# Gating the w_in quarters on early loads, moving the scalars to ScalarE's queue, moving column sum and bias add to GpSimd, and scheduling for longer DMA transposes in a fused linear-attention and StarReLU kernel

## Chip, cores and metric

One core of one Trainium2 chip. The metric is the device time of one execution in microseconds (us). "Fast" and "slow" are states of a run: a run is called slow when it is over 1.5% above the fastest of the same kernel.

## The reference, cut

```python
for t in range(S):                      # B, H, S, D = 4, 8, 768, 48
    state = alpha[:, :, t, :, None] * state + k_t (outer) v_t
    y[:, :, t] = q_t @ state
x = y.transpose(0, 2, 1, 3).reshape(B * S, H * D)        # 3072 x 384
h = x @ w_in                                              # 384 -> 2048
g = s * relu(h) ** 2 + b
out = g @ w_out                                           # 2048 -> 384
```

## The kernel before

The 3072 rows are 24 blocks of 128. Per block: alpha, q, k, v are loaded, log decay is summed on TensorE (PE), q and k are scaled and transposed, scores are masked, and y is formed and transposed into `xd`. Blocks are gathered in groups; a unit is one PSUM bank of up projection (`mm1`) or a quarter of a block's down projection (`mm2`). Both s and b stay out of the big products: `oevac` multiplies by s and adds `bias_w`, which is b times the column sum of w_out.

A list scheduler in Python, with assumed durations, decides the order in which every engine's instructions are emitted. The engines then run in that order. The parts that matter:

```python
GROUPS = [1, 1, 2, 2, 2, 4, 4, 4, 4]     # blocks per group
LEAD = 24.0                              # how far attention runs ahead, in units
N_PE_T = 10                              # blocks 0..9 transpose on PE, the rest by DMA
LOADS = ["b0", "i0", "i1", "b1", "i2", "i3", "b2", "o0", "o1", "o2", "o3", "b3"]
...
def colsum_part(i):
    nc.vector.tensor_tensor(out=colpart if i else colsum, ...)   # 128x768 float32
...
# scalars b and s: issued on GpSimd's DMA queue, behind the four w_in quarters
op("POOL", 0.7, t + 30, lambda: nc.gpsimd.dma_start(out=b_col, ...), w=["b"], lat=2.0)
op("POOL", 0.8, -5, bias_mul, r=["b"], w=["bones"])
...
# DMA transposes of q and k, and of y, with the scheduler's assumed times
op("SP", 0.5, -3000, st_Tdma, n, r=[("qb", i3), ("kb", i3)], w=[("qkT", i3)], lat=1.2, dma=1.1)
op("SP", 0.5, -3000, st_yTdma, n, r=[("yn", i3)], w=[xd], lat=1.2, dma=0.5)
...
op("DVE", 0.54, t + 0.1, oevac, x, r=[o, "bias", "s"], w=[("os", (x // 4) % 3)], drop=o)
```

## Time and profile before

| | before |
|---|---|
| time, median (3 runs) | 205.95 us (205.75 to 206.21) |
| span of the profiled run | 204.4 us |
| PE busy / idle | 167.6 / 36.8 us |
| DVE, ACT, POOL busy | 131.7, 107.8, 39.7 us |

PE idle of a stretch is its length minus PE's busy time there; the prediction gives it by stretch. DVE is VectorE, ACT ScalarE, POOL GpSimd, SP SyncE.

### The profile page before, as it was taken

To read this page: it belongs to the slowest core of one execution; us is meant where nothing else is said; L and a number is where in the kernel's file an instruction comes from. 1 tells how busy PE (TensorE), PEld (TensorE's weight loads), DVE (VectorE), ACT (ScalarE), POOL (GpSimd) and SP (SyncE) were. 2 spreads that over 40 slices of the span, in tenths; PEclk is the share of its full clock that TensorE was granted. 3 is DMA by queue.
4 is the path that set the end of the run, shared out by engine and by line. 5 is a ranking of instruction groups with operands and counts; after the bars stand their busy time and mean duration, and the time that the engine had idled before them with its cause. 6 is when DMAs were issued, how large, how long until landed. Compare 5 with 4: busy or idle time off the path is not lost.

```text
span 204.4 us, 4279 instructions
## 1 busy us (share of the span) xinstructions
PE 167.6 (82%) x1594; PEld 107.4 (53%) x1594; DVE 131.7 (64%) x240; ACT 107.8 (53%) x235; POOL 39.7 (19%) x76
## 2 busy tenths in 40 slices
PE   1301966897999999897789978897969999999993
PEld 0201954656887887663355544454536555555661
DVE  3501299979999998967567857776757544444321
ACT  4100689836897677643746856557445444444100
POOL 8403034124104530031223100321202000000000
PEclk9999999999999999999999999999999999999999
DMA  6999999999999999999999799999964221111122
GB/s 131 175 189 195 270 379 209 188 209 227 189 211 188 216 205 191 188 211 178 159 224 184 148 204 206 176 204 209 201 138 109 61 59 40 40 42 38 38 77 77
DMA packets 127701, 33.64 MB, mean 165 GB/s; under 512 B 121024, under 2 KB 127680, under 8 KB 127680
## 3 DMA queue, kind: packets, MB, share of 16 engines
q1 hardware_dynamic: 126016, 31.80, 75.3%
q0 software_dynamic: 1664, 1.57, 4.8%
q8 instruction: 12, 0.20, 0.4%
q14 instruction: 9, 0.07, 0.1%
HBM read 25.17 MB, written 4.72 MB: 146 GB/s over the span
## 4 chain that ended last, share of the span: by engine, by line
PE 56%; DMA 26%; DVE 7%; issue 4%; POOL 3%; ACT 3%; SPq 0%; POOLq 0%; ACTq 0%; DVEq 0%
PE bank L530 23%; PE bank L502 22%; DMA qkT<-qk 19%; DMA b_col<-in_moe_b_dram 6%; PE a_ps L417 3%; PE bank L353 2%; POOL w_in_bf L255 2%; DMA a_in<-in_alpha_dram 1%; PE bank L450 1%; DVE colpart L272 1%; DVE am L426 1%; PE bank L309 1%; PE bank L376 1%; ACT r L511 1%; DVE gt L523 1%
## 5 line engine op out<-in xcount | busy, mean ns | idle before, releaser
L502 PE MATMUL bank<-xd,w_in_bf 128*128 128x512 bf16 (+2 forms) x432 | 76.5, 315 | 0.7 <-DMA xd<-yn 0.5
L511 ACT ACTIVATE r<-bank 128x512 bf16<-128x512 f32 x96 | 56.6, 604 | 35.7 <-PE bank L502 26.7
L530 PE MATMUL bank<-w_out_bf,gt 128*128 128x384 bf16 x384 | 73.7, 326 | 0.0
L523 DVE TENSOR_TENSOR gt<-r 128x512 bf16<-128x512 bf16 x96 | 41.9, 448 | 23.7 <-ACT r L511 23.3
L530 PEld LDWEIGHTS <-gt 128*128 128x128 bf16 x384 | 35.7, 98 | 25.3 <-issue 0.2
L502 PEld LDWEIGHTS <-w_in_bf 128*128 128x128 bf16 x432 | 38.2, 101 | 18.8 <-issue 1.4
L426 DVE TENSOR_TENSOR am<-a_ps,mask 128x1024 bf16<-128x1024 f32 x24 | 29.3, 1219 | 11.7 <-PE a_ps L417 11.5
L406 POOL TENSOR_TENSOR s_st<-t,blast 64x192 bf16<-64x192 bf16 x32 | 19.3, 603 | 43.7 <-PE bank L442 11.7
L330 POOL CAST vb<-v_in 128x384 bf16<-128x384 f32 x24 | 13.1, 546 | 61.3 <-DMA v_in<-in_v_dram 29.8
L539 DVE SCALAR_TENSOR_TENSOR o_sb<-bank,s_col,bias_w 128x384 f32<-128x384 f32 x24 | 14.7, 613 | 13.9 <-PE bank L530 13.9
L302 ACT ACTIVATE la<-a_in 128x384 bf16<-128x384 f32 x24 | 12.7, 530 | 18.4 <-DMA a_in<-in_alpha_dram 18.4
L463 ACT ACTIVATE yn<-bank 128x384 bf16<-128x384 f32 x24 | 11.9, 496 | 17.8 <-PE bank L450 17.7
L417 PE MATMUL a_ps<-qkT 64*128 64x128 bf16 x192 | 9.7, 222 | 10.6 <-DMA qkT<-qk 9.1
L333 DVE TENSOR_TENSOR qk<-q_in,b_s 128x384 bf16<-128x384 f32 x24 | 13.9, 579 | 4.3 <-ACT b_s L323 4.3
L323 ACT ACTIVATE b_s<-bank 128x384 f32<-128x384 f32 x24 | 11.8, 491 | 7.5 <-PE bank L314 6.8
L376 PE MATMUL bank<-vb,qk 128*128 128x96 bf16 x80 | 6.8, 209 | 10.7 <-POOL vb L330 10.7
L341 DVE TENSOR_TENSOR qk<-k_in,binv 128x384 bf16<-128x384 f32 x24 | 14.4, 598 | 0.4 <-DMA k_in<-in_k_dram 0.4
L417 PEld LDWEIGHTS <-qkT 64*128 64x128 bf16 x192 | 5.5, 95 | 15.7 <-DMA qkT<-qk 12.0
L309 PE MATMUL bank<-la,U_bf 128*128 128x384 bf16 x24 | 8.2, 340 | 4.9 <-ACT la L302 4.9
L450 PE MATMUL bank<-vb,am 128*128 128x48 bf16 x192 | 8.9, 185 | 3.8 <-DVE am L426 3.8
L326 ACT ACTIVATE binv<-bank 128x384 f32<-128x384 f32 x24 | 11.9, 494 | 0.0
L376 PEld LDWEIGHTS <-qk 128*128 128x128 bf16 x80 | 4.9, 99 | 12.8 <-issue 10.8
(42 smaller groups left out, 106.5 us busy)
## 6 DMA issues: line engine op xcount, KB each, us to landing
a_in<-in_alpha_dram SPq DMA_DIRECT2D x24, 192.0 KB, 3.8
q_in<-in_q_dram SPq DMA_DIRECT2D x24, 192.0 KB, 3.7
k_in<-in_k_dram SPq DMA_DIRECT2D x24, 192.0 KB, 3.7
v_in<-in_v_dram SPq DMA_DIRECT2D x24, 192.0 KB, 3.8
out_dram<-o_sb SPq DMA_DIRECT2D x24, 192.0 KB, 2.2
wst<-in_moe_w_out_dram SPq DMA_DIRECT2D x4, 768.0 KB, 8.3
w_in_bf<-in_moe_w_in_dram POOLq DMA_DIRECT2D x4, 384.0 KB, 9.5
qkT<-qk SPq DMA_TRANSPOSE x14, 3.8
```

The costliest lines, as they stand in the source:

```text
L330: nc.gpsimd.tensor_copy(out=vb_sb[n % 3], in_=v_in[n % NIN])
L333: nc.vector.tensor_tensor(out=qk_sb[n % 3][:, 0, :, 0:D], in0=q_in[n % NIN], in1=b_sb[n % 2], op=ALU.mult,)
L341: nc.vector.tensor_tensor(out=qk_sb[n % 3][:, 1, :, 0:D], in0=k_in[n % NIN], in1=binv_sb[n % 2], op=ALU.mult,)
L376: nc.tensor.matmul(out=p_ps[:, p, :], lhsT=kb[:, 128 * p : 128 * p + 128], rhs=vb[:, 96 * p : 96 * p + 96], start=True, stop=True,)
L406: nc.gpsimd.tensor_tensor(out=s_sb[n % 2][rows, :, cols], in0=t1_sb[n % 2][rows, :, cols], in1=blast_sb[n % 2][rows].unsqueeze(2).to_broad ...
L417: nc.tensor.matmul(out=a_ps[:, e, p, :], lhsT=qkT[64 * e : 64 * e + 64, 1, p, :], rhs=qkT[64 * e : 64 * e + 64, 0, p, :], start=True, stop ...
L426: nc.vector.tensor_tensor(out=am_sb[n % 2].rearrange("a e p t -> a (e p) t"), in0=a_ps.rearrange("a e p t -> a (e p) t"), in1=mask.unsquee ...
L502: nc.tensor.matmul(out=hp[:, i * n : (i + 1) * n], lhsT=w_in_bf[:, kk, 128 * j : 128 * (j + 1)], rhs=xd_sb[g % 3][:, kk, 0:n], start=(kk = ...
L511: nc.scalar.activation(out=r_sb[w % 2], in_=bank("h", w), func=AF.Relu)
L523: nc.vector.tensor_tensor(out=dst, in0=r, in1=r, op=ALU.mult)
L530: nc.tensor.matmul(out=op[:, 0:d_model], lhsT=gt_sb[:, slot, j, :], rhs=w_out_bf[:, j, :], start=(j == 0), stop=(j == NJ - 1),)
L539: nc.vector.scalar_tensor_tensor(out=out_sb[(x // 4) % 3], in0=bank("o", x // 4)[:, 0:d_model], scalar=s_col, in1=bias_w, op0=ALU.mult, op ...
```

## The change

The intent is to fill PE's empty start: let the narrow loads that attention needs go first, let w_in follow when they have landed, take the scalars out of w_in's queue, unload DVE, and let the scheduler assume longer DMA transposes. Two more blocks are transposed on PE, and one group of two blocks becomes two groups of one. The diff, cut:

```diff
-GROUPS = [1, 1, 2, 2, 2, 4, 4, 4, 4]
-LEAD = 24.0
+GROUPS = [1, 1, 2, 1, 1, 2, 4, 4, 4, 4]
+LEAD = 28.0
-N_PE_T = 10
+N_PE_T = 12
+AFTER = ['k0', 'q1', 'k2', 'k2']
+N_POOL_BIAS = 12
+NOUT = 4
+TLAT = 3.0
-LOADS = ["b0", "i0", "i1", "b1", "i2", "i3", "b2", "o0", "o1", "o2", "o3", "b3"]
+LOADS = 'a0 q0 k0 v0 a1 q1 k1 v1 a2 q2 k2 a3 q3 k3 v2 v3 o0 o1 o2 o3 a4 q4 k4 v4'
...
+    nc.scalar.dma_start(out=b_col, in_=moe_b.to_broadcast((128, 1)))
+    nc.scalar.dma_start(out=s_col, in_=moe_s.to_broadcast((128, 1)))
...
+    def touch(what):                       # waits on GpSimd for a load
+        src = tensors[what[0]][1][what[1]]
+        nc.gpsimd.tensor_copy(out=touch_sb, in_=src[:, 0, 0:1])
...
-        nc.vector.tensor_tensor(            # column sum
+        nc.gpsimd.tensor_tensor(
...
+    def oscale(x): nc.scalar.activation(out=out_sb[...], in_=bank("o", x // 4)[...], func=AF.Copy, scale=s_col)
+    def obias(x): nc.gpsimd.tensor_tensor(out=o_sb, in0=o_sb, in1=bias_w, op=ALU.add)
...
+        op("POOL", 0.06, -3000 + i, touch, x, r=[x], w=[("touch", i)])
+        op("POOL", 0.9, -3000 + i, load_w_in, i, r=[("touch", i)], w=[("wib", i)], lat=1.2, dma=2.3)
...
-                   lat=1.2, dma=1.1)        # st_Tdma
+                   lat=TLAT, dma=1.6)
-                op("SP", 0.5, -3000, st_yTdma, n, r=[("yn", i3)], w=[xd], lat=1.2, dma=0.5)
+                op("SP", 0.5, -3000, st_yTdma, n, r=[("yn", i3)], w=[xd], lat=TLAT, dma=0.7)
```

The first 12 evacuations become `oscale` and `obias`; the other 12 stay on DVE. The rest of the diff adds a fourth output buffer and tunes assumed durations and the scheduler's own model of the queues.

More of the change, by code (lines that the diff above doesn't have):

```diff
@@ L81, in run, with since, u_eng @@
         until = {}
-        queue = 0.0
+        queue = soft = 0.0
+        flying = []
         todo = n
+        def since(u):
+            a = 0.0
+            for d in self.ops[u][5]:
+                same = self.ops[d][0] == self.ops[u][0]
+                x = end[d] + (0.0 if same and u_eng(u) == "PE" else self.ops[d][6])
+                a = max(a, x + (0.0 if same and self.ops[d][7] is None else self.HOP))
+            return a
+        def u_eng(u):
+            return self.ops[u][0]
         def start(a, i):
@@ L108, in run @@
                 free[e] = end[i] = t + dur
+            elif eng == "POOL":
+                free[e] = t + dur
+                at = max(t + 1.3, soft)
+                soft = end[i] = at + dma
+                flying = [x for x in flying if end[x] > at]
+                for x in flying:
+                    end[x] += dma
+                queue = max(queue, at) + dma
+                for e2, items in ready.items():
+                    ready[e2] = [(since(x), x) for _, x in items]
             else:
@@ L111, in run @@
                 end[i] = queue
+                flying.append(i)
                 free[e] = max(t + dur, queue - self.BACKLOG)
@@ L127, in run @@
                 if not left[u]:
-                    a = 0.0
-                    for d in self.ops[u][5]:
-                        same = self.ops[d][0] == self.ops[u][0]
-                        x = end[d] + (0.0 if same and eng == "PE" else self.ops[d][6])
-                        a = max(a, x + (0.0 if same else self.HOP))
-                    ready[self.ops[u][0]].append((a, u))
+                    ready[u_eng(u)].append((since(u), u))
         self.begin, self.end = begin, end
@@ L235 @@
     gt_sb = sb.tile([128, RING, NJ, C], BF16, name="gt")
-    out_sb = many("o_sb", 3, [128, d_model], FP32)
+    out_sb = many("o_sb", NOUT, [128, d_model], FP32)
     w_in_bf = sb.tile([128, 3, d_ff], BF16, name="w_in_bf")
@@ L243 @@
     colpart = sb.tile([128, 2 * d_model], FP32, name="colpart")
+    touch_sb = sb.tile([128, 1], FP32, name="touch")
     bones = sb.tile([128, 128], FP32, name="bones")
@@ L279, in colsum_add @@
     def colsum_add():
-        nc.vector.tensor_tensor(out=colsum, in0=colsum, in1=colpart, op=ALU.add)
+        nc.gpsimd.tensor_tensor(out=colsum, in0=colsum, in1=colpart, op=ALU.add)
     def bias_mul():
@@ L539, in oevac @@
         nc.vector.scalar_tensor_tensor(
-            out=out_sb[(x // 4) % 3],
+            out=out_sb[(x // 4) % NOUT],
             in0=bank("o", x // 4)[:, 0:d_model],
@@ L549, in ostore, with oscale, obias @@
         n = x // 4
-        nc.sync.dma_start(out=out[n * C : (n + 1) * C, :], in_=out_sb[(x // 4) % 3])
+        nc.sync.dma_start(out=out[n * C : (n + 1) * C, :], in_=out_sb[(x // 4) % NOUT])
+    def oscale(x):
+        nc.scalar.activation(
+            out=out_sb[(x // 4) % NOUT],
+            in_=bank("o", x // 4)[:, 0:d_model],
+            func=AF.Copy,
+            scale=s_col,
+        )
+    def obias(x):
+        o_sb = out_sb[(x // 4) % NOUT]
+        nc.gpsimd.tensor_tensor(out=o_sb, in0=o_sb, in1=bias_w, op=ALU.add)
     sched = Schedule(len(banks), {"c": 2, "T": 1, "P": 2, "y": 2, "Y": 1, "h": 3, "o": 2, "b": 1})
@@ L557, in want @@
         return (4 * n - LEAD) * UNIT
-    loads = LOADS + [f"b{n}" for n in range(NBLK) if f"b{n}" not in LOADS]
-    early = {0: [], 1: []}
-    for rank, item in enumerate(loads):
-        t, i = rank - 1000, int(item[1:])
-        if item[0] == "i":
-            op("POOL", 0.9, t, load_w_in, i, w=[("wib", i)], lat=1.2, dma=2.3)
-        elif item[0] == "o":
-            op("SP", 0.5, t, load_w_out, i, w=[("wst", i)], lat=1.2, dma=2.2)
+    loads = LOADS.split()
+    for n in range(NBLK):
+        loads += [x for x in (f"{y}{n}" for y in "aqkv") if x not in loads]
@@ L567 @@
+    tensors = {"a": (alpha, a_in), "q": (q, q_in), "k": (k, k_in), "v": (v, v_in)}
+    ranks = {}
+    for rank, item in enumerate(loads):
+        x, i = item[0], int(item[1:])
+        ranks[x, i] = rank - 1000
+        if x == "o":
+            op("SP", 0.5, rank - 1000, load_w_out, i, w=[("wst", i)], lat=1.2, dma=2.2)
             for e in range(2):
                 op("ACT", 0.78, -400, cast_w_out, i, e, r=[("wst", i)], w=[("wob", i, e)])
-            op("DVE", 0.85, -5, colsum_part, i, r=[("wst", i)],
+            op("POOL", 1.3, -2, colsum_part, i, r=[("wst", i)],
@@ L570 @@
                w=["colpart" if i else "colsum"])
             if i:
-                op("DVE", 0.85, -5, colsum_add, r=["colpart"], w=["colsum"])
-        elif i == 0:
-            for x, (name, src, dst) in enumerate(
-                (("a", alpha, a_in), ("q", q, q_in), ("k", k, k_in), ("v", v, v_in))
-            ):
-                op("SP", 0.45, t + 0.1 * x, load, 0, src, dst, w=[(name, 0)], lat=1.2, dma=0.98)
-            op("POOL", 0.7, t + 30,
-               lambda: nc.gpsimd.dma_start(out=b_col, in_=moe_b.to_broadcast((128, 1))),
-               w=["b"], lat=2.0)
-            op("POOL", 0.7, t + 30,
-               lambda: nc.gpsimd.dma_start(out=s_col, in_=moe_s.to_broadcast((128, 1))),
-               w=["s"], lat=2.0)
-            op("POOL", 0.8, -5, bias_mul, r=["b"], w=["bones"])
+                op("POOL", 1.3, -2, colsum_add, r=["colpart"], w=["colsum"])
@@ new lines, in block_loads @@
+    def block_loads(n):
+        for x, (src, dst) in tensors.items():
+            op("SP", 0.45, ranks[x, n], load, n, src, dst, w=[(x, n % NIN)], lat=1.2, dma=0.98)
+    for n in range(4):
+        block_loads(n)
+    for i in range(4):
+        x = AFTER[i][0], int(AFTER[i][1:])
+        op("POOL", 0.06, -3000 + i, touch, x, r=[x], w=[("touch", i)])
+        op("POOL", 0.9, -3000 + i, load_w_in, i, r=[("touch", i)], w=[("wib", i)], lat=1.2, dma=2.3)
+    op("POOL", 0.8, -5, bias_mul, r=[("S", 0)], w=["bones"])
@@ L595 @@
             t = want(n)
-            if n:
-                rank = loads.index(f"b{n}") - 1000
-                for x, (name, src, dst) in enumerate(
-                    (("a", alpha, a_in), ("q", q, q_in), ("k", k, k_in), ("v", v, v_in))
-                ):
-                    op("SP", 0.45, rank + 0.1 * x, load, n, src, dst, w=[(name, ii)],
-                       lat=1.2, dma=0.98)
+            if n >= 4:
+                block_loads(n)
             op("ACT", 0.43, t - 1.0, st_ln, n, r=[("a", ii)], w=[("la", i2)])
@@ L608 @@
             op("POOL", 0.6, t + 0.2, st_vcast, n, r=[("v", ii)], w=[("vb", i3)])
-            op("DVE", 0.47, t + 0.2, st_qb, n, r=[("q", ii), ("b", i2)], w=[("qb", i3)])
-            op("DVE", 0.47, t + 0.2, st_kb, n, r=[("k", ii), ("bi", i2)], w=[("kb", i3)])
+            op("DVE", 0.52, t + 0.2, st_qb, n, r=[("q", ii), ("b", i2)], w=[("qb", i3)])
+            op("DVE", 0.52, t + 0.2, st_kb, n, r=[("k", ii), ("bi", i2)], w=[("kb", i3)])
             if n < N_PE_T:
@@ L613 @@
                    take=("T", n))
-                op("DVE", 0.61, t + 0.4, st_Tcopy, n, r=[("T", n)], w=[("qkT", i3)], drop=("T", n))
+                op("DVE", 0.66, t + 0.4, st_Tcopy, n, r=[("T", n)], w=[("qkT", i3)], drop=("T", n))
             else:
                 op("SP", 0.5, -3000, st_Tdma, n, r=[("qb", i3), ("kb", i3)], w=[("qkT", i3)],
-                   lat=1.2, dma=1.1)
+                   lat=TLAT, dma=1.6)
             if not last:
@@ L628 @@
             op("PE", 0.33, t + 0.5, st_A, n, r=[("qkT", i3)], w=["a"], lat=0.27)
-            op("DVE", 1.15, t + 0.6, st_mask, n, r=["a"], w=[("am", i2)])
+            op("DVE", 1.2, t + 0.6, st_mask, n, r=["a"], w=[("am", i2)])
             rr = [("am", i2), ("qkT", i3), ("vb", i3)] + ([] if first else [("S", 1 - i2)])
@@ L646 @@
             t = w * UNIT
-            op("PE", 0.66, t, mm1, w,
+            op("PE", {1: 0.76, 2: 0.71, 4: 0.66}[m], t, mm1, w,
                r=[("xd", g % 3, x) for x in range(m)] + [("wib", j0 // 4)],
                w=[("h", w)], lat=0.27, take=("h", w))
-            op("ACT", 0.5, t + 0.5, relu, w, r=[("h", w)], w=[("r", w % 2)], drop=("h", w))
+            op("ACT", 0.51, t + 0.5, relu, w, r=[("h", w)], w=[("r", w % 2)], drop=("h", w))
             op("DVE", 0.36, t + 1.0, square, w, r=[("r", w % 2)],
@@ L663 @@
             if jq == 3:
-                op("DVE", 0.54, t + 0.1, oevac, x, r=[o, "bias", "s"],
-                   w=[("os", (x // 4) % 3)], drop=o)
-                op("SP", 0.5, -2000, ostore, x, r=[("os", (x // 4) % 3)], dma=0.55)
+                os = ("os", (x // 4) % NOUT)
+                if x // 4 < N_POOL_BIAS:
+                    op("ACT", 0.38, t + 0.1, oscale, x, r=[o], w=[os], drop=o)
+                    op("POOL", 0.7, t + 0.1, obias, x, r=["bias"], w=[os])
+                else:
+                    op("DVE", 0.58, t + 0.1, oevac, x, r=[o, "bias"], w=[os], drop=o)
+                op("SP", 0.5, -2000, ostore, x, r=[os], dma=0.55)
     sched.emit()
```

## The prediction

> **What bounds the kernel now.** I began with the page's first part. TensorE (PE) is busy 167.6 us of a 204.4 us span and its clock is granted in full, so the span is 167.6 us of PE work plus 36.8 us in which PE stands still. No other engine comes near (VectorE, DVE, has 131.7 us). The question is therefore where those 36.8 us lie and which of them the change takes away.
>
> Second, the table of busy time in stretches of 5 us (columns: stretch, its length, then PE, PEld, DVE, ACT, POOL busy with counts, granted clock, DMA share, GB/s):
>
> ```profile
> 5.00:10.00 5.00, 1.68 (x16) 1.13 (x17) 2.94 (x4) 0.79 (x3) 2.63 (x5) 1.00 1.12 175
> 10.00:15.00 5.00, 0.00 (x0) 0.00 (x0) 0.00 (x0) 0.00 (x0) 0.00 (x0) 1.00 1.21 189
> 15.00:20.00 5.00, 0.80 (x12) 0.66 (x11) 0.26 (x1) 0.04 (x1) 1.58 (x3) 1.00 1.04 194
> ...
> 70.00:75.00 5.00, 5.00 (x58) 3.97 (x57) 5.00 (x9) 3.36 (x9) 2.79 (x6) 1.00 0.97 209
> ...
> 100.00:105.00 5.00, 3.49 (x29) 1.80 (x28) 3.06 (x6) 2.03 (x4) 0.67 (x2) 1.00 1.09 202
> ...
> 165.00:170.00 5.00, 5.00 (x29) 2.62 (x28) 2.23 (x5) 2.20 (x5) 0.00 (x0) 1.00 0.11 41
> ```
>
> Adding five minus PE busy over all stretches gives PE idle of 17.0 us in 0 to 20, 6.6 us in 20 to 50, 0 in 50 to 85, 9.8 us in 85 to 155 and 3.5 us after that (the last evacuation and store). The reader should see that from 10 to 15 us every engine is idle while the DMA engines are full. The tail from 155 is pure PE work, so time saved earlier arrives at the end almost one for one.
>
> Third, the chain of waits says why (start, length, what):
>
> ```profile
> 6.29 11.52 DMA b_col<-in_moe_b_dram
> 17.99 0.61 POOL bones L284
> 18.60 0.48 POOL vb L330
> 19.12 0.48 PE bank L376 x4
> ...
> 38.06 0.88 DVE colpart L272
> 38.96 0.97 DVE colsum L280
> 40.06 1.53 PE bank L290 x4
> ```
>
> A load of 0.5 KB, the scalar b, takes 11.5 us. GpSimd (POOL) waits for it in program order to scale `bones`, and the cast of v for block 0 stands behind that. Later the column sum on DVE, seven instructions of about 0.94 us, ends at 39.9 us and PE waits for it before the bias matmul.
>
> Fourth, the DMA view of single issues in that stretch (last column: us from issue to landing):
>
> ```profile
> v_in<-in_v_dram SPq DMA_DIRECT2D x1, 192.0 KB, 6.0
> w_in_bf<-in_moe_w_in_dram POOLq DMA_DIRECT2D x1, 384.0 KB, 6.6
> a_in<-in_alpha_dram SPq DMA_DIRECT2D x1, 192.0 KB, 11.2
> b_col<-in_moe_b_dram POOLq DMA_DIRECT2D x1, 0.5 KB, 11.5
> ```
>
> Block 0's v was issued at 2.66, so it landed at 8.7 us, and nobody used it until 18.6. The four quarters of w_in were issued at 3.0 to 5.5 and landed at about 9.6, 12.6, 15 and 17.5. b_col stood behind all four in one ring. Meanwhile alpha of block 1 needed 11.2 us, where the first load needed 2.9.
>
> Fifth, the waits of PE in 85 to 155 us (us in total, times, longest):
>
> ```profile
> PEld L417 <- DMA qkT<-qk: 12.0, 9, 2.0
> PE a_ps L417 <- DMA qkT<-qk: 9.1, 9, 1.6
> ```
>
> Nearly all of that 9.8 us is one kind of wait: the score matmuls stand in PE's order sooner than the DMA transpose lands (median 3.8 us after issue, longest 5.6), though other matmuls were ready behind them.
>
> **What the Trainium skill says.** "DMA: Bandwidth & Descriptors", section "Queues, rings and completion order": each DMA engine goes round the rows that have work, one packet at a time. The trace agrees that rings share: the w_in quarters kept landing 2.4 to 3 us apart while loads of 192 KB crawled. A scalar in ScalarE's (ACT) own row should thus not wait for megabytes. "GPSIMD Engine Reference", section 3.1: a two-input elementwise instruction runs at about 2.6 cycles per element at 1.2 GHz, 2.2 ns. The trace's `s_st` products of 192 elements take 603 ns, which is 2.2 ns each and some 0.18 us fixed. "ScalarE: Activation LUTs", section "What ACT_TABLE_LOAD costs": a per-partition scale operand adds about 93 ns. This trace has no such ACTIVATE; 0.50 us for the 128x384 eviction gives an estimate of 0.59. "TensorE: Matmul & The Clock Gate", Part 1: after idling, PE runs at half rate until some 3.4 us of sustained work. The trace agrees: the first 36 narrow matmuls of the up projection took 3.96 us (0.11 each), a later 24 took 1.50 (0.063).
>
> **The change part by part.**
>
> (1) The scalars go to ACT's queue, issued behind the table load that ends at 2.0 us. By the 2.9 us of a first load they land near 5, so `bones` is done near 6 and v of block 0 is cast at about 8 at latest instead of 18.6. Block 0's path then is as before from the cast on: 18.57 to the copy of xd ending at 21.53, 3 us. So xd of block 0 is ready at 11 to 12 us: 10 us earlier.
>
> (2) The w_in quarters now wait for k0, q1, k2, k2. k0 landed at 5.4, so the first quarter is issued near 6 instead of 3.0 and, with 6.6 us to landing, is there at 12 to 12.5; the first up projection starts then, 9 us earlier. But the rest comes late. A quarter is about 2.45 us of DMA time (4.8% of the span on its queue over four), a load 0.98 (192 KB at 200 GB/s). The second quarter lands near 15 to 16. k2 lands near 17, so quarters three and four land near 22 and 25 (before: all by 17.5). In the new PE order the third and fourth units of block 0 stand behind work that needs v2, which lands near 24. PE therefore idles again between about 16 and 25. By 25 us PE will have done some 10 us of work: 15 us idle, against 17 before by 21.6.
>
> (3) Interleaving puts blocks 0 to 3 ahead of w_out: 16 loads of 0.98 and 9.8 us of w_in from 2.7 on end at 28.2 instead of 24.3, so the quarters of w_out land near 30, 32, 34 and 37 (before: 26.3 to 33.2), 4 us later. PE has blocks 0 to 3 to fill this with. I count about 2.5 us of further idle between 25 and 42.
>
> (4) Column sum on POOL: seven additions of 128x768 at 0.18 + 768 x 2.2 ns = 1.87 us (estimate; 13 us in all), beginning when the first w_out quarter lands at 30, with a state update of 1.2 us between them: done near 44.5. PE reaches the bias matmul near 42.5. A stall of 0 to 2 us takes the place of waits for DVE. DVE loses 6.9 us of work.
>
> (5) Twelve evacuations move from DVE (0.61) to ACT (0.59) and POOL (0.18 + 384 x 2.2 ns = 1.0). ACT rises to about 115 us, POOL to about 65, DVE falls to about 118. None of these is the bound.
>
> (6) Smaller groups: 8 units at 0.75 instead of 0.66 us, +0.7. Two more blocks transposed on PE: 2 x (0.46 + 0.17) = +1.2. PE work becomes 169.5 us. Four DMA transposes fewer.
>
> (7) Scheduling with a longer assumed transpose and a larger lead moves the score matmuls later in PE's order. I expect the 9.8 us of idle to fall to about 4.
>
> The sum: 169.5 work + 15 idle to 25 us + 2.5 to 42 + 1.5 for the bias and until 50 + 4 in the middle + 3.5 at the end = 196.0 span. The measured time is 1.55 us above the span (205.95 against 204.4), so about **197.5 us**, 4% less than before. As a check by units at 50 us: before has done 16 units of projection (8 up, 8 down) of 192; I count 26 for the changed kernel, 6.5 us ahead, of which (6) takes 1.9; the middle adds 5.8; 205.95 - 4.6 - 5.8 = 195.6.
>
> **The rivals.** First, the late weights eat the whole start: w_in and w_out land 8 and 4 us later, and DMA already looked full from 5 to 150 us. For it speaks the DMA share of 1.0. Against it speaks that PE is not short of attention work then, and that narrow loads rather than weights were starving it. If the start gained nothing and only the middle did, the time would be about 202. Second, the middle does not improve because the SyncE queue is the limit: each transpose occupies it for 1.2 to 2.6 us, loads and stores stand behind in order, and the stores now also wait for POOL. Then the front's gain comes back as waits for transposes or loads, and the time is 201 to 204. Third, POOL becomes the wait: the column sum shares memory ports with DVE and holds casts of v and state updates back; at 3 us per addition the bias would come at 52 us and cost 8, giving 204. Fourth, it goes better than I count: quarters land sooner, the bias is hidden and the middle loses almost nothing, giving 191 to 193.
>
> **Range and chances.** Each rival alone still ends near or below 204, since the 10 us hole is certainly closed and only part of it can be lost again. The 8 in 10 range is 192.5 to 203.5. The 2% line is at 201.8; I give 0.84 to faster, 0.14 to within 2%, 0.02 to slower.
>
> **What would show it.** In the changed profile: b_col landing within 4 us and no stretch of 5 us without PE work before 25 us except around 17 to 24 (step 1, 2); first up projection at 12 to 13 us; w_out's last quarter at about 37 (3); POOL additions at 1.3 to 1.9 us and PE's wait before the bias under 2.5 us (4); `o_sb` ACTIVATE near 0.59 (5); PE busy near 169.5 (6); PE's waits for qkT below 5 us in total (7). I am wrong if PE idle before 50 us stays above 21 us, or if waits for qkT or for inputs between 50 and 155 us stay near 10.

## More of the kernel before

The prediction shows the lines on which this rests. One more becomes important later: the logarithm of block 1's alpha, ACT's first use of that load (start, length, engine, line, operation, and in brackets, where there is one, idle time before it and what ended it):

```profile
20.34 0.51 ACT L302 ACTIVATE la<-a_in 128x384 bf16<-128x384 f32 x1
```

## The result

The changed kernel took 199.07 us (median of 4, 198.21 to 200.28) against 206.05 (median of 4) for the kernel before. A ratio here is the mean time of one kernel's fast runs over that of the other's of the same rounds, so it is not quite the ratio of the medians: it is 0.9667, 95% interval 0.9605 to 0.9729. The time lies in the predicted range, 1.6 us above the point.

| | before | after |
|---|---|---|
| span | 204.4 | 198.0 |
| PE busy / idle | 167.6 / 36.8 | 173.1 / 24.9 |
| PE idle in 0-20 | 17.0 | 10.4 |
| 20-50 | 6.6 | 8.4 |
| 50-85 | 0 | 1.8 |
| 85-155 | 9.8 | 0.3 |
| 155-end | 3.5 | 4.0 |

PE idle fell by 11.9 us, PE busy time rose by 5.5: 6.4 us of span. The profile after, stretches of 5 us with the columns of the prediction's table:

```profile
10.00:15.00 5.00, 2.87 (x29) 2.48 (x30) 2.45 (x3) 0.98 (x2) 0.50 (x1) 1.00 1.24 220
15.00:20.00 5.00, 3.57 (x53) 2.79 (x51) 2.89 (x5) 3.15 (x8) 2.71 (x6) 1.00 0.87 172
20.00:25.00 5.00, 1.18 (x22) 0.85 (x20) 3.26 (x6) 1.48 (x5) 0.27 (x1) 0.89 1.16 178
25.00:30.00 5.00, 4.12 (x42) 4.11 (x42) 1.25 (x2) 0.19 (x1) 2.01 (x4) 0.50 1.11 333
...
45.00:50.00 5.00, 3.00 (x8) 1.45 (x9) 4.29 (x7) 1.30 (x3) 2.77 (x3) 0.78 0.97 191
...
100.00:105.00 5.00, 5.00 (x48) 2.84 (x46) 4.37 (x7) 2.97 (x8) 2.31 (x4) 1.00 0.91 117
```

The empty stretch from 10 to 15 us has work in it and 100 to 105 is full. New holes stand at 20 to 25 and 45 to 50, and each is followed by a granted clock (third from last) below 1. The chain of waits names the two holes:

```profile
18.01 7.26 DMA v_in<-in_v_dram
26.36 1.28 PE bank L531 x12
...
43.13 1.88 POOL colpart L301
45.08 1.88 POOL colsum L309
46.99 2.14 PE bank L319 x4
```

The load of v of block 2 is late, and PE waits 4.1 us for its cast. Then the column sum on POOL is late and PE waits 3.0 us for it. PE in order of time:

```profile
11.26 0.50 PE L479 MATMUL bank<-vb,am 128*128 128x48 bf16 x8 [1.89 <-DVE am L455]
...
25.89 0.48 PE L405 MATMUL bank<-vb,qk 128*128 128x96 bf16 x4 [4.08 <-POOL vb L359]
26.16 1.48 PE L531 MATMUL bank<-xd,w_in_bf 128*128 128x128 bf16 x12
...
32.42 0.83 PE L531 MATMUL bank<-xd,w_in_bf 128*128 128x128 bf16 x12
...
46.99 2.14 PE L319 MATMUL bank<-colsum,bones 128*128 128x384 f32 x4 [3.02 <-POOL colsum L309]
```

The first 12 narrow up projections after the first wait took 1.48 us (the chain counts 1.28 of it, from the end of the instruction before); by 32.42 us 12 of them took 0.83. The granted clock does not show every slow stretch: in the kernel before it read 1.00 in 20 to 25 us while narrow matmuls took 0.11 us each instead of 0.063; here it read 0.50 for about the same (1.28 us for 12, 0.107 each). The groups of instructions that moved:

```profile
L582 ACT ACTIVATE o_sb<-bank,s_col x12: 572/588/606, 42.8 to 137.2; 128x384 f32<-128x384 f32 x12
L591 POOL TENSOR_TENSOR o_sb<-o_sb,bias_w x12: 994/1000/1424, 49.9 to 137.9; 128x384 f32<-128x384 f32 x12
...
L301 POOL TENSOR_TENSOR colpart<-wst x3: 1810/1868/1877, 35.4 to 43.1; 128x768 f32<-128x768 f32 x3
```

The three numbers after the colon are the least, median and longest duration in ns. PE's own waits from 50 to 160 us, where before had 9.1 us of waits for `qkT`:

```profile
PE bank L405 <- DVE qk L370: 1.2, 1, 1.2
PE bank L531 <- DVE o_sb L568: 0.3, 1, 0.3
PE a_ps L446 <- DVE qkT L389: 0.2, 1, 0.2
```

### The profile page after: what moved, and what is told of

It is laid out like the page before. It is cut to its first block, busy times and chain, and to the rows that moved or that the text cites. A ratio compares the mean times of both kernels' runs of the same rounds, so it can differ in the third digit from the quotient of the medians.

```text
span 198.0 us, 4422 instructions
## 1 busy us (share of the span) xinstructions
PE 173.1 (87%) x1664; PEld 111.3 (56%) x1664; DVE 130.1 (66%) x223; ACT 114.1 (58%) x249; POOL 66.2 (33%) x97
## 4 chain that ended last, share of the span: by engine, by line
PE 62%; SPq 11%; DVE 8%; POOL 6%; DMA 6%; issue 3%; ACT 1%; DVEq 0%; POOLq 0%
PE bank L531 25%; PE bank L559 24%; SPq L274 9%; DMA v_in<-in_v_dram 4%; POOL colsum L309 3%; POOL colpart L301 3%; DMA k_in<-in_k_dram 3%; PE a_ps L446 3%; PE bank L382 2%; DVE am L455 2%; PE bank L479 2%; PE bank L405 1%; DVE qk L370 1%; DVE gt L552 1%; PE bank L338 1%
## 5 line engine op out<-in xcount | busy, mean ns | idle before, releaser
L531 PE MATMUL bank<-xd,w_in_bf 128*128 128x128 bf16 (+2 forms) x480 | 75.2, 303 | 0.8 <-DMA w_in_bf<-in_moe_w_in_dram 0.5
L559 PE MATMUL bank<-w_out_bf,gt 128*128 128x384 bf16 x384 | 71.9, 328 | 0.6 <-ACT w_out_bf L298 0.5
L552 DVE TENSOR_TENSOR gt<-r 128x512 bf16<-128x512 bf16 x96 | 48.4, 520 | 25.3 <-ACT r L540 24.9
L531 PEld LDWEIGHTS <-w_in_bf 128*128 128x128 bf16 x480 | 39.8, 103 | 20.4 <-DMA w_in_bf<-in_moe_w_in_dram 0.7
L359 POOL CAST vb<-v_in 128x384 bf16<-128x384 f32 x24 | 15.4, 642 | 32.6 <-DMA v_in<-in_v_dram 26.5
L331 ACT ACTIVATE la<-a_in 128x384 bf16<-128x384 f32 x24 | 12.7, 531 | 11.7 <-DMA a_in<-in_alpha_dram 11.7
L362 DVE TENSOR_TENSOR qk<-q_in,b_s 128x384 bf16<-128x384 f32 x24 | 15.7, 656 | 4.9 <-ACT b_s L352 4.8
L591 POOL TENSOR_TENSOR o_sb<-o_sb,bias_w 128x384 f32<-128x384 f32 x12 | 12.5, 1043 | 12.2 <-ACT o_sb L582 9.8
L568 DVE SCALAR_TENSOR_TENSOR o_sb<-bank,s_col,bias_w 128x384 f32<-128x384 f32 x12 | 7.4, 615 | 13.6 <-PE bank L559 13.6
L492 ACT ACTIVATE yn<-bank 128x384 bf16<-128x384 f32 x24 | 11.9, 497 | 5.8 <-PE bank L479 5.6
L428 DVE TENSOR_TENSOR t<-bank,s_st 128x384 bf16<-128x384 f32 x16 | 8.8, 551 | 7.0 <-PE bank L405 5.0
L382 PE MATMUL bank<-ident_bf,qk 128*128 128x128 bf16 x96 | 9.9, 250 | 1.6 <-DVE qk L362 1.2
```

The costliest lines, as they stand in the source:

```text
L359: nc.gpsimd.tensor_copy(out=vb_sb[n % 3], in_=v_in[n % NIN])
L362: nc.vector.tensor_tensor(out=qk_sb[n % 3][:, 0, :, 0:D], in0=q_in[n % NIN], in1=b_sb[n % 2], op=ALU.mult,)
L382: nc.tensor.transpose(out=t_ps[:, x, p, :], in_=f[:, 128 * p : 128 * p + 128], identity=ident_bf,)
L531: nc.tensor.matmul(out=hp[:, i * n : (i + 1) * n], lhsT=w_in_bf[:, kk, 128 * j : 128 * (j + 1)], rhs=xd_sb[g % 3][:, kk, 0:n], start=(kk = ...
L552: nc.vector.tensor_tensor(out=dst, in0=r, in1=r, op=ALU.mult)
L559: nc.tensor.matmul(out=op[:, 0:d_model], lhsT=gt_sb[:, slot, j, :], rhs=w_out_bf[:, j, :], start=(j == 0), stop=(j == NJ - 1),)
```

## Experiments

Every edit here changes what the scheduler sees, so the order of other instructions moves with it; a run therefore tells what a part is worth inside its kernel and not alone. Twelve kernels ran, all correct. Kernels named b_ start from the kernel before, a_ from the changed one. Sets of four shared a chip and 7 runs of the kernel before, whose medians were 209.22 us (b_scalars, b_tlat, a_dvecol, a_v2), 205.87 (a_again, a_tlat, a_lead, a_v2dve) and 205.74 (a_groups, a_dveout, a_ungated, b_npet). The changed kernel unaltered ran only in the second set.

### b_scalars: the scalars alone

```diff
+    nc.scalar.dma_start(out=b_col, in_=moe_b.to_broadcast((128, 1)))
+    nc.scalar.dma_start(out=s_col, in_=moe_s.to_broadcast((128, 1)))
-            op("POOL", 0.7, t + 30, lambda: nc.gpsimd.dma_start(out=b_col, ...), w=["b"], lat=2.0)
-            op("POOL", 0.7, t + 30, lambda: nc.gpsimd.dma_start(out=s_col, ...), w=["s"], lat=2.0)
```

> The kernel before with one part alone: the two scalars loaded on ScalarE's queue. My ledger of PE idle: b_col lands near 5 us, v of block 0 is cast near 8, the first up projection starts near 12 to 13 instead of 21.6, but alpha, q, k, v of block 1 still land only at 15 to 19 us behind w_in, so block 1 is hardly earlier. Expected: PE idle in 0 to 20 us falls from 17.0 to about 13, the 9.8 us in 85 to 155 stay, time 202 to 204 (about 3 us better). Rival A (the 10 us hole is the whole gain): time near 196 to 198. Rival B (weights bound the start, the hole is free): 205 to 206.5.

Ratio 1.0005 (0.9886 to 1.0124). This is rival B: no gain was seen, although v of block 0 was cast at 12.2 us instead of 18.6. Its profile fell on a slow run, so its stages are not compared; the order of events in it stands. Alpha of block 1 still reached ACT only at 17.2 us. Closing the named 10 us wait exposed a second one standing just behind it. In this slow run PE idle was 4.3 us less up to 50 us than in the kernel before and 4.7 us more from 50 to 155, so the start may have gained and the middle lost it again; a slow run cannot settle that.

### a_ungated: w_in at once

```diff
-        op("POOL", 0.06, -3000 + i, touch, x, r=[x], w=[("touch", i)])
-        op("POOL", 0.9, -3000 + i, load_w_in, i, r=[("touch", i)], w=[("wib", i)], lat=1.2, dma=2.3)
+        op("POOL", 0.9, -3000 + i, load_w_in, i, w=[("wib", i)], lat=1.2, dma=2.3)
```

> The changed kernel with the quarters of w_in issued at once, near 3 us, instead of after k0, q1, k2, k2. Theory 1 (order among loads only moves the hole): w_in lands at 9.6 to 18, block 1's loads at 15 to 19 instead of 9 to 13; PE idle in 0 to 20 us rises from 10 to 13 or 14, idle in 20 to 50 falls from 8.4 to 4 to 6 because quarters three and four are early and v2 comes earlier; time within 1% of the changed kernel, ratio 0.955 to 0.972. Theory 2 (the gate is worth the hole): idle in 0 to 50 us rises by 3 us or more, ratio 0.975 to 0.985.

Ratio 0.9884 (0.983 to 0.9937), 202.57 us: worse than the changed kernel, by more than Theory 1 allowed and nearly as Theory 2 said. PE idle in 0 to 50 us is 22.4 (16.4 and 6.1) against 18.8 in the changed kernel, a rise of 3.6. The line that decides it is block 1's alpha on ACT, first in the changed kernel:

```profile
7.69 0.52 ACT L331 ACTIVATE la<-a_in 128x384 bf16<-128x384 f32 x1 [1.42 <-DMA a_in<-in_alpha_dram]
```

and then ungated:

```profile
17.29 0.52 ACT L331 ACTIVATE la<-a_in 128x384 bf16<-128x384 f32 x1 [11.02 <-DMA a_in<-in_alpha_dram]
```

With w_in in flight from 3 us, the 192 KB of alpha issued at 4.01 took 13.2 us to land; gated, issued at 3.97, it took 3.6. PE's order has block 1's work ahead of block 0's up projection, so all of it waits. Without the gate the start keeps 1.1 us of the 4.7 us of idle that it had gained (22.4 and 18.8 against 23.5 before). The gate was tested only by taking it away; scalars and gate alone on the kernel before were not run.

### b_tlat: the transposes' assumed times alone

```diff
-                   lat=1.2, dma=1.1)        # st_Tdma
+                   lat=3.0, dma=1.6)
-    ... st_yTdma ... lat=1.2, dma=0.5)
+    ... st_yTdma ... lat=3.0, dma=0.7)
```

> The kernel before with only the scheduler's assumed times of the DMA transposes raised (latency 1.2 to 3.0, queue time 1.1 to 1.6 and 0.5 to 0.7); no instruction is added or taken away, only the order moves. My ledger: the score matmuls stand later in PE's order, PE idle in 85 to 155 us falls from 9.8 to 1 to 3, the start stays as it was, time 197.5 to 200. Rival (the SyncE queue limits the middle): the idle comes back as waits for loads or for transposes and the time is 204 to 206.

Ratio 0.9779 (0.9699 to 0.9858), 203.9 us: unclear at the 2% line, and later than the 197.5 to 200 expected. The stages on my ledger did not come out: PE idle in 85 to 155 us fell only from 9.8 to 8.4. The waits for `qkT` vanished and others took their place, at the product of k and v (L376) and at the sum of the log decay (L309):

```profile
PE bank L376 <- POOL vb L330: 3.9, 3, 2.4
PE bank L376 <- ACT r L511: 2.1, 2, 1.5
PE bank L309 <- ACT r L511: 1.0, 1, 1.0
```

The ratio looks better than the trace; the kernel before was slow and scattered on this chip (207.0 to 212.1), which may be the reason. In the trace the span is 203.0 against 204.4, the 1.4 us that the stage shows. This is the prediction's second rival in part.

### a_tlat: the same times set back in the changed kernel

```diff
-TLAT = 3.0
+TLAT = 1.2
-                   lat=TLAT, dma=1.6)
+                   lat=TLAT, dma=1.1)
-    ... st_yTdma ... lat=TLAT, dma=0.7)
+    ... st_yTdma ... lat=TLAT, dma=0.5)
```

> The changed kernel with only the assumed times of the DMA transposes set back (latency 3.0 to 1.2, queue time 1.6 to 1.1 and 0.7 to 0.5). Theory 1 (my prediction's step 7: these times alone empty the middle): the waits for qkT return, PE idle in 85 to 155 us rises from 0.3 to 7 to 10, time 205 to 207, ratio about 1.0. Theory 2 (the first run of this part alone on the kernel before moved the waits from qkT to the casts of v and left 8.4 of 9.8 us: the lead, the smaller groups and the unloaded VectorE do the rest): idle 2 to 5 us, time 200 to 203, ratio 0.97 to 0.985.

Four runs of 202.32, 204.48, 207.42 and 208.51 us, the last two slow, so there is no ratio: unclear in time. PE idle in 85 to 155 us is 5.9 us, between the two theories' ranges, and its cause is the old one:

```profile
PE a_ps L446 <- DMA qkT<-qk: 4.6, 6, 1.3
```

By the idle of this one profile the longer times are needed in the changed kernel, and by b_tlat they are not enough in the kernel before.

### a_lead: the lead set back

```diff
-LEAD = 28.0
+LEAD = 24.0
```

> The changed kernel with the lead of the attention set back from 28 to 24 units. Theory 2 (the lead is what lets the middle absorb late loads of v): PE idle in 50 to 155 us rises from 2.1 to 5 to 8, time 202 to 205, ratio 0.98 to 0.995. Theory 1 (the transposes' assumed times are enough): idle there stays at 2 to 3 us, ratio 0.96 to 0.973.

PE idle from 50 to 155 us is 2.3 us, as with the larger lead. The lead is not what empties the middle; that part of Theory 2 falls. The ratio 0.9662 (0.9582 to 0.9742) overlaps the control's on the same chip, so no worth of the lead was shown.

### a_again: the changed kernel as control

No edit.

> The changed kernel unaltered, as a control on the chip of these four runs: the chip of the first four runs gave the kernel before 3 us more than the chip of the prediction. Expected: ratio to before 0.96 to 0.973 as measured first; PE idle as first: some 10, 8, 2, 0.5 and 4 us in 0 to 20, 20 to 50, 50 to 85, 85 to 155 and after. If the chip matters, the ratio leaves this interval.

Ratio 0.9576 (0.9518 to 0.9635), 197.31 us; slightly below the interval expected, so the chip, or the round, moves the ratio by about 1%. Idle by stage repeats: 10.0, 8.2, 1.8, 0.8 and 4.0 us. PE busy was 171.0 instead of 173.1: the same 3.0 us wait before the bias matmul was followed here by a bias matmul of 1.56 us, there of 2.14.

### a_groups: groups and PE transposes set back

```diff
-GROUPS = [1, 1, 2, 1, 1, 2, 4, 4, 4, 4]
+GROUPS = [1, 1, 2, 2, 2, 4, 4, 4, 4]
-N_PE_T = 12
+N_PE_T = 10
```

> The changed kernel with the groups and the count of blocks transposed on PE set back ([1,1,2,2,2,4,4,4,4] and 10 instead of 12). So far: the transposes' assumed times are needed (set back, 5.9 us of waits for qkT return) but not sufficient on the kernel before (8.4 us stay, as waits on v), and the lead does nothing for the middle. Theory P (the four DMA transposes fewer on the SyncE queue, for blocks 10 and 11, free it for the loads of v): PE idle in 50 to 155 us rises from 2.1 to 5 to 9, and PE work falls by 1.9 us, time 200 to 204, ratio 0.97 to 0.99. Theory Q (evacuations off VectorE free the middle): idle stays at 1 to 3 us and the time falls to 195 to 198, ratio 0.95 to 0.965.

Ratio 0.9914 (0.985 to 0.9978), 203.49 us. PE idle from 50 to 155 us rises to 6.3 us, with waits for the DMA transpose of y and for v:

```profile
PE bank L531 <- DMA xd<-yn: 2.1, 1, 2.1
PE bank L405 <- POOL vb L359: 2.1, 2, 1.2
```

Theory P's idle is met, and its time; the ratio lies a little above its range. PE busy did not fall by 1.9 us as it said: it was 173.7 us, against 173.1 and 171.0 in the two profiles of the changed kernel. Two settings moved together here, so this run alone does not say which.

### b_npet: assumed times and two more blocks transposed on PE

```diff
-N_PE_T = 10
+N_PE_T = 12
(and the edit of b_tlat)
```

> The kernel before with the transposes' assumed times raised and 12 instead of 10 blocks transposed on PE. Theory P: beside the assumed times it takes the four DMA transposes fewer; PE idle in 85 to 155 us falls from 8.4 (assumed times alone) to 1 to 4, PE work rises by 1.2 us, time 198 to 201, ratio 0.96 to 0.975. Theory Q: it stays at 6 to 9 us and the ratio at 0.98 to 0.99.

Ratio 0.9797 (0.9722 to 0.9873), 200.73 us. PE idle in 85 to 155 us is 3.75 us against 8.4 with the assumed times alone. Theory P's idle, between its 1 and 4, and its time of 198 to 201, though not quite its ratio (unclear at the 2% line):

```profile
85.00:155.00 70.00, 66.25 (x590) 37.32 (x597) 52.00 (x96) 41.41 (x93) 14.48 (x25) 1.00 0.88 179
```

With this most of the middle's gain is reproduced on the kernel before by two settings; no work is moved but the transposes of two blocks. Nothing was done for the start here, yet the median is 5.0 us below that of the kernel before on this chip; the whole change took 7.0 and 8.6 us off in its two sets. The profiled span is 198.6 us, against 198.0 with the whole change: PE idle is 30.8 us instead of 24.9, but PE busy is 167.8 instead of 173.1. So about half of the gain in time or more can be had from the middle alone, and much of what the filled start wins in idle is lost again in PE's busy time. The parts do not simply add: a_ungated has the full gain of the middle (2.2 us of idle from 50 to 155 us) and its ratio is 0.9884.

### a_dveout: all evacuations on DVE

```diff
-N_POOL_BIAS = 12
+N_POOL_BIAS = 0
```

> The changed kernel with all 24 evacuations on VectorE as before, none on ScalarE and GpSimd. Theory Q (the moved evacuations are part of what empties the middle): PE idle in 50 to 155 us rises from 2.1 to 5 to 8, time 201 to 204. Theory P (they are off the path, as no engine but PE is near its limit): idle 1 to 3 us, but the first evacuations now wait for the bias, which GpSimd finishes near 47 us; time 196 to 200, ratio 0.955 to 0.97.

Ratio 0.9674 (0.9596 to 0.9751), 198.92 us; PE idle from 50 to 155 us is 3.2 us, just above Theory P's range and well below Theory Q's; 2.6 of it lie after 85 us, where the changed kernel has 0.3. Moving 12 evacuations off DVE was not shown to be worth anything.

### a_dvecol: column sum back on DVE

```diff
-        nc.gpsimd.tensor_tensor(            # colsum_part and colsum_add
+        nc.vector.tensor_tensor(
-            op("POOL", 1.3, -2, colsum_part, ...
+            op("DVE", 0.85, -5, colsum_part, ...
```

> The changed kernel with the column sum back on VectorE (0.94 us an addition instead of 1.87). My ledger: PE's 3.0 us wait before the bias matmul and the slow clock after it (granted 0.78 in 45 to 50 us) go, time 194.5 to 197, ratio to the changed kernel 0.98. Rival: the seven additions delay VectorE's squares and masks between 30 and 45 us as much as they save, time 198 to 200.

Ratio 0.9564 (0.9461 to 0.9668), 200.01 us where the kernel before took 209.22. PE no longer waits before the bias matmul, which starts at 43.2 us instead of 47.0, and PE idle in 20 to 50 us is 5.6 instead of 8.4. The wait is thus put down to POOL. But PE idle from 50 to 155 us rose from 2.1 to 4.0, and the ratio overlaps both of the changed kernel's (it is 0.989 and 0.999 of them, where 0.98 was expected), so no gain in time is shown.

### a_v2 and a_v2dve: v of block 2 earlier, alone and with the column sum on DVE

```diff
-LOADS = '... a2 q2 k2 a3 q3 k3 v2 v3 ...'
+LOADS = '... a2 q2 k2 v2 a3 q3 k3 v3 ...'
```

> The changed kernel with v of block 2 loaded right after k of block 2, ahead of alpha, q, k of block 3. My ledger: v2 lands near 21 instead of 25, PE's 4.1 us wait for the cast of v2 shrinks to at most 1.5 us and the clock falls less (granted 0.50 in 25 to 30 us), time 195 to 197. Rival (the late quarters of w_in, landing at 25.5 and 27, bound this stretch): PE waits for w_in instead and the time stays at 198 to 200.

Ratio 0.9655 (0.9567 to 0.9743). The 4.1 us wait for the cast of v2 is gone (0.36 us is left, at the cast for block 3), yet the bias matmul started only 1.75 us earlier:

```profile
45.24 2.93 PE L319 MATMUL bank<-colsum,bones 128*128 128x384 f32 x4 [3.18 <-POOL colsum L309]
```

The bias wait is not all that took the gain: PE idle from 50 to 155 us rose from 2.1 to 5.1, 2.7 of it waits for casts of v.

> The changed kernel with both repairs: v of block 2 loaded before block 3, and the column sum on VectorE. Alone the first gave 0.9655 (its gain was swallowed by a 3.2 us wait before the bias matmul) and the second 0.9564. If that swallowing is right, together they remove both waits: PE idle in 20 to 50 us falls from 8.4 to 2 to 4, time 192.5 to 195.5, ratio 0.935 to 0.95. Rival (the gain comes back later as waits for loads, because DMA sets the pace): idle in 50 to 155 us rises to 5 or more and the ratio stays at 0.955 to 0.965.

Ratio 0.9569 (0.9491 to 0.9647), against 0.9576 for the changed kernel on the same chip: the combined repair gave nothing that these runs can see. Its profile fell on a slow run and is not compared. The rival's ratio was met; whether for the rival's reason stays open, but a_v2 and a_dvecol also came back with more idle in the middle. No version tried is shown to beat the changed kernel.

## Why the prediction was right, and where its steps missed

The direction, the size and the ledger held: 26.5 us of PE idle predicted, 24.9 measured; 169.5 us of PE work predicted, 173.1 (171.0 in the control) measured. That the span came within 2.0 us is in part luck: from 50 to 155 us the idle was 1.9 us less than said and PE work 3.6 us more, while the start (18.8 us of idle to 50 us, 19.0 said) and the end (4.0, 3.5 said) came out nearly as summed. The check by units did not hold: 26 units of projection were counted by 50 us, and the trace has 21 (13 up, 8 down) against 16 before. Step by step:

1. **Scalars.** b_col landed at 4.0 us and v of block 0 was cast at 6.96, both sooner than said; the load was issued at 0.75 us, during the table load and not behind it. But xd of block 0 was ready at 13.4 us (11 to 12 said) and the first up projection began at 14.0 (12 to 13 said). "As before from the cast on" failed: before, the scores were masked at 9.8 us, long before v was cast at 18.6; now y waited for the mask until 11.2. And "10 us earlier" was credited to the wrong part: alone, the move gave 1.0005. I saw that alpha of block 1 took 11.2 us behind w_in and did not draw the conclusion.
2. **Gate.** The landings were close: first quarter at 12.7 us (12 to 12.5 said), second at 16.2 (15 to 16), third at 25.5 (22), fourth at 27.7 (25), and PE idle up to 25 us was 14.2 (15 said). I booked the gate as a cost that delays weights; ungating costs 3.6 us of idle in 0 to 50 us, so the start does not open without it.
3. **w_out.** POOL got its first quarter at 30.6 us and the last landed at 37.0, near the 30 and 37 said. PE idle from 25 to 50 us was 4.5 (4.0 said).
4. **Column sum.** 1.81 to 1.94 us an addition (1.87 said). It ended at 46.9 instead of 44.5, also because POOL stood 1.7 us at the state update between, waiting for DVE; PE waited 3.0 us instead of "0 to 2". The third rival had the kind of loss right and its size too large.
5. **Evacuations.** 0.588 us on ACT and 1.00 on POOL, as said: "GPSIMD Engine Reference", section 3.1, and "ScalarE: Activation LUTs", section "What ACT_TABLE_LOAD costs", were right for the new work (1.87 and 1.00 us for 768 and 384 elements; 0.588 us is 0.09 above the eviction of the same size without a scale operand, 0.497). ACT and POOL totals were 114.1 and 66.2, as said. DVE was missed: 130.1 instead of about 118, because single DVE instructions stretched. The square of 128x512 kept its median of 0.42 us, but its mean rose from 448 to 520 ns and its longest from 0.76 to 2.03 us. This goes with work on POOL: the 63 squares that ran beside no POOL instruction took 0.43 us at most, and the longest ran beside the column sum's additions; with those back on DVE (a_dvecol) the longest square was 1.23 us. What the two engines share is not shown. The changed kernel's list of PE's waits has none for a square.
6. **PE work.** The term that was mis-sized: +1.9 us said, +5.5 measured. After its two new waits PE ran its matmuls at about half rate (clock 0.50 in 25 to 30 us). The timeline has three units of up projection at 1.48, 1.49 and 1.07 us instead of 0.83, eight transposes at 1.06 instead of 0.62, the bias at 2.14 instead of 1.53 and four down projections at 1.49 instead of 0.81: 3.3 us in sum, which with the 1.9 us of new work as predicted accounts for nearly all. I had noted that PE is slow at first and did not apply it to waits that I predicted myself.
7. **The middle.** Idle of 9.8 us was to fall to 4 and fell to 0.3, plus 1.8 new between 50 and 85. The reason given was incomplete. The longer assumed times only moved the waits from `qkT` to v (b_tlat, 8.4 us left). Together with two more blocks transposed on PE, 3.75 us were left; what takes the rest is not shown. The lead does nothing here. Why four DMA transposes fewer matter so much was not tested by itself; that they free SyncE's in-order queue for the loads of v is an inference from which waits appear and vanish.

The first rival, that late weights eat the start, was wrong in the main: sent early, the weights cost 3.6 us more of idle. But late quarters may have cost too: three and four were issued at 18.7 and 19.5 us, and the load of v of block 2, issued at 18.01, took 7.3 us beside them where the gated alpha of block 1 took 3.6; PE's 4.1 us wait is for it. In the second rival one reading was short: in the kernel before, SyncE took 1.2 to 3.6 us over a transpose, not 1.2 to 2.6. Not tested by themselves were the order of the loads, the smaller groups, the fourth output buffer and the scheduler's model of the queues.

## What to carry to other kernels

When the chain of waits shows one long wait, ask what would be waited for if it were gone; the load next in line may be held by the same traffic. In these runs wide transfers on a second queue starved narrow ones (13.2 us instead of 3.6 for 192 KB), so hold the wide ones until the narrow ones that the first work needs have landed. Allow for more than the length of a wait on PE: matmuls were slow after most of the long waits here. Count also what a part brings in time and not only in idle: the start was the plan, and the middle alone brings about half of the gain or more. And in a statically ordered kernel, test an assumed latency together with the queue that has to serve it.

## What the Trainium skill lacked or had wrong

- "DMA: Bandwidth & Descriptors", section "Queues, rings and completion order": packet-wise rounds between rows are described, but not how unequal the split becomes. With the w_in quarters in flight, a load of 192 KB took 11.2 and 13.2 us instead of 3.6, while the quarters kept landing 2.4 to 3 us apart. The page gives no warning that a cast load on GpSimd's queue starves narrow loads on SyncE's.
- "TensorE: Matmul & The Clock Gate", Part 1: after an idle window of about 3.4 us PE falls to half rate, says the page, which also calls the window free-running. Here shorter waits were enough in some runs: after 3.02 us the four bias matmuls took 2.14 us and after 3.18 us (a_v2) 2.93, while in another run of the changed kernel (a_again) they took 1.56 after 3.00 us.
